# A kernel of attention and a gated product: seven products also in the fourth stay, and kept weight pieces loaded back

## The chip, the cores and the metric

The kernel runs on one core of one Trainium2 chip. The time is the device time of one execution in microseconds. Every number of a profile comes from one profiled execution; it lists the engines TensorE (PE, with its weight loads as PEld), VectorE (DVE), ScalarE (ACT), GpSimd (POOL) and SyncE (SP), whose queue issues nearly all DMAs.

## The reference, cut to what matters

Attention with batch 4, 8 heads, 768 positions and 64 channels a head; a query sees 8 global keys and the last 96 positions, with a bias that falls with the distance. Its result, as 3072 rows x of 512 channels, goes through two products that are multiplied and a third:

```python
scores = scale * np.matmul(q, k.transpose(0, 1, 3, 2)) + bias
a = softmax(np.where(keep, scores, -1e9))
x = matmul(a, v).transpose(0, 2, 1, 3).reshape(3072, 512)
out = (x @ w_a) * (x @ w_b) @ w_out      # w_a, w_b: 512 x 1536; w_out: 1536 x 512
```

The three weights are float64, whose words the kernel turns into float32 on the chip. The products are made in a split form: each float32 operand is cut into a high half that the matmul takes whole and a low half that is the rest, and three matmuls (high x high, low x high, high x low) stand for one product.

## The kernel before, in words

**Tiles.** The 3072 rows are six blocks u of 512. The 1536 inner channels are six sets fp of 256. A set has six pieces of 128 x 512: A11, A12, A21, A22 (columns of w_a and w_b) and O0, O1 (rows of w_out). Attention of a block runs in four granules (scores, exponentials, turned weights through DRAM, values).

**Stays and passes.** Converted weights of a few sets are kept in SBUF for a stay, and blocks pass by them. STAYS and TURNS give 18 passes: stay 1 (sets 0, 1, 2; passes 0 to 2, blocks 0, 1, 2), stay 2 (3, 4; passes 3 to 6), stay 3 (5; passes 7 to 9), stay 4 (sets 5, 2; passes 10, 11, 12 with blocks 3, 4, 5), stay 5 (3, 4; passes 13, 14), stay 6 (0, 1; passes 15 to 17). The sums of a block so far are stored to DRAM (`part`) and loaded when it comes again. Blocks 4 and 5 have none yet in passes 11 and 12.

**A pass.** In the first stay `project_plain` makes the two inner products as they are. From the second on `project` uses a seven-product scheme (Strassen's, in Winograd's form) on quarters of x and of A: seven products of 12 matmuls of 256 columns on the two PSUM banks al and ga, with copies and sums between them on ScalarE and VectorE. Their product h (two tiles of 128 x 512) goes back through w_out. In passes 0 to 12 `back` does it plainly: `cut` makes the halves hh and hl of both tiles (two copies, two subtractions, 512 wide), and 8 x 3 matmuls of 512 columns a set add up in the four banks acc; `evict` takes them out once a pass, with four sums or, for a block with no sums yet, four copies. In passes 13 to 16 (PAIRED), `project(strong=True)` calls `seven`, which makes seven forms of h, each a high and a low part of 256 columns, and four sums between quarters; `strong_back` then does seven products of six matmuls of 256 columns for each set of the pass, on three banks, and adds them to the four quarters of the block's sums, a VectorE sum behind each product. Pass 17 has its own end.

**Where the forms lie.** `room` gives tiles of attention and of the conversions, which are idle by pass 13, to the forms of h (hroom) and of w_out (wroom). `load_o` loads O0 and O1 of a set back and makes seven forms of them. For sets in QUADFPS, `load_w` leaves the O pieces to `load_o`.

**Weights.** `to32` makes a float32 piece of a float64 one: a DMA of 512 KB from wts, two ScalarE operations (L688, L723) and four VectorE operations (L695, L703, L713, L730), into a tile m of which each tag has one copy. For the first stay, `convert_plain` converts the six pieces of sets 0, 1, 2 and splits them straight into their places (`wform` with direct). For later stays `convert` converts all six pieces of a set again, makes the sums S1 to S4 and stores A11, A12, S2, S1, S3, S4, A22, O0, O1 to DRAM (dw); `load_w` loads them (wl) when the stay begins, and splits them. So sets 0, 1 and 2 are converted twice.

**Order.** The plan records every operation, and `order` emits them in the order of ORDER, a list of indices written out in the code. An operation that either engine can do runs on ScalarE where ON_SCALAR names it, else on VectorE. Each engine and SP's queue work through their own operations strictly in this order, and an operation waits for the last user of its tile or bank.

Of the kernel before, what the change touches and what calls it, by code (L numbers as in the profile page):

```python
# [10 lines left out]
F32 = mybir.dt.float32  # L11
F32R = mybir.dt.float32r
# [67 lines left out]
PAIRED = (13, 14, 15, 16)  # L80
LAST = len(PASSES) - 1
QUADFPS = (3, 4, 0, 1)
SEVEN = {13: ("psS", "acc0", "psA"), 14: ("acc1", "acc2", "acc3"), 15: ("psS", "acc0", "psA"), 16: ("acc1", "acc2", "acc3"), 17: ("psS", "acc3", "psA")}
# [15 lines left out]
ROOMAT = 13  # L99
LASTFP = 1  # L100
OADJ = {4: (26612.0, 23990.0), 5: (41063.0, 32495.0)}
BADJ = {13: (-88541.0, -44480.0), 14: (-15687.0, -31498.0), 15: (-69190.0, 137971.0), 16: (-1031.0, -17073.0), 17: (8575.0, 2763.0, 3140.0)}
# [503 lines left out]
class Fast:  # L606
# [144 lines left out]
    def wform(self, fp, name, due, src, direct):  # L751
        if direct:
            w = self.slot(fp, name, 0.0, True)
            self.split(due, lambda: src[:, :], w, lambda: w[:, 1], lambda: w[:, 0], CN, [src])
            return
# [4 lines left out]
    def convert(self, fp, due, step, direct):  # L760
# [5 lines left out]
        def quad(i, name):  # L766
            m[name] = self.to32(fp, i, at[i], "m" + name)
# [1595 lines left out]
```

## Time and profile before

| | |
|---|---|
| median of 3 runs | 688.73 us (687.43 to 692.22) |
| profiled execution | 689.54 us, span 687.8 us |
| TensorE, VectorE, ScalarE busy | 668.1, 636.7, 381.9 us |
| matmuls | 6519 |
| moved by DMA | 164.80 MB |

The span runs from the first to the last instruction; 1.74 us of the execution lie around it. "Busy" counts the time in which at least one instruction of the engine is under way. A matmul's own duration is longer than its distance to the next one, since matmuls are pipelined.

### The profile page before, as it was taken

How to read it: one execution, taken by the hardware profiler on the slowest of the kernel's cores; microseconds unless marked ns; L12 is line 12 of the kernel's file. 1: busy time of each engine (PE TensorE's matmuls, PEld its weight loads, DVE VectorE, ACT ScalarE, POOL GpSimd, SP SyncE). 2: the span in 40 equal slices, each digit the busy share in tenths (PEclk: the TensorE clock that was granted, in tenths of full speed). 3: DMA queues.
4: the chain of work that ended last, by engine and by line, in shares of the span. 5: the costliest groups of instructions: out<-in, count | busy, mean ns of one | idle time of the engine just before them, and what ended most of it. 6: DMA issues, size and time to landing. Idle time of an engine off the chain costs nothing.

```text
span 687.8 us, 17093 instructions
## 1 busy us (share of the span) xinstructions
PE 668.1 (97%) x6519; PEld 606.6 (88%) x6519; DVE 636.7 (93%) x1616; ACT 381.9 (56%) x1029; POOL 10.0 (1%) x32
## 2 busy tenths in 40 slices
PE   5899999999999999999999999999999999999996
PEld 4689797778887999989999998999999999999996
DVE  8999899878799999999989998999989999999996
ACT  8999767564635666634756665344444554554210
POOL 1000000000000000000000000000000000000000
PEclk9999999999999999999999999999999999999999
DMA  8769899989999978899888979966566537522334
GB/s 304 254 227 286 277 260 322 286 272 272 319 277 317 328 233 251 286 280 296 312 268 240 304 245 283 302 239 241 186 226 198 187 108 230 179 69 77 108 108 128
DMA packets 79100, 164.80 MB, mean 240 GB/s; under 512 B 8034, under 2 KB 32738, under 8 KB 77218
## 3 DMA queue, kind: packets, MB, share of 16 engines
q1 hardware_dynamic: 78722, 163.41, 74.6%
q8 instruction: 53, 0.87, 0.5%
q14 instruction: 37, 0.30, 0.1%
q10 hardware_dynamic: 288, 0.22, 0.1%
HBM read 110.65 MB, written 52.95 MB: 238 GB/s over the span
## 4 chain that ended last, share of the span: by engine, by line
PE 77%; DMA 9%; DVE 9%; ACT 3%; issue 1%; SPq 1%; DVEq 0%; ACTq 0%
PE al L1403 21%; PE acc L1593 17%; PE ga L1403 16%; PE m_acc L1650 3%; PE ps L1031 3%; DMA wl_A<-dw_A 2%; PE m_psS L1650 2%; DMA py<-mir 2%; DMA wr<-wts 2%; PE pa L515 2%; DMA X<-dx 1%; ACT t L1015 1%; PE ps_al L515 1%; PE m_psA L1650 1%; DVE t L999 1%
## 5 line engine op out<-in xcount | busy, mean ns | idle before, releaser
L1593 PE MATMUL acc<-w_O,hh 128*128 128x512 f32 x416 | 148.4, 401 | 0.0
L1015 ACT ACTIVATE t<-t,sm 128x168 f32<-128x168 f32 x192 | 81.9, 429 | 29.4 <-DVE sm L999 29.4
L1593 PEld LDWEIGHTS acc<-w_O,hh 128*128 128x128 f32 x416 | 78.2, 188 | 16.1
L1593 PE MATMUL acc<-w_O,hl 128*128 128x512 f32 x208 | 81.9, 394 | 0.0
L1403 PE MATMUL al<-xf_T,w_S 128*128 128x256 f32 x600 | 79.5, 282 | 0.0
L1403 PEld LDWEIGHTS al<-xf_T,w_S 128*128 128x128 f32 x600 | 75.7, 188 | 1.4 <-ACT s L650 0.2
L999 DVE CUSTOM_DVE_ANT_0 t<-ps,mask 128x168 f32<-128x168 f32 x168 | 49.2, 326 | 8.3 <-PE ps L1031 8.1
L650 ACT COPY s<-al 128x512 f32<-128x512 f32 x49 | 28.7, 586 | 49.2 <-PE al L1403 49.1
L688 ACT ACTIVATE wm<-wr 128x512 f32<-128x512 f32 x54 | 35.8, 671 | 15.2 <-DMA wr<-wts 6.8
L1593 PEld LDWEIGHTS acc<-w_O,hl 128*128 128x128 f32 x208 | 39.2, 188 | 5.6 <-DVE hl L660 0.4
L1031 PEld LDWEIGHTS ps<-qk 64*64 64x64 f32 x1008 | 30.6, 139 | 14.8 <-issue 6.6
L1403 PE MATMUL al<-xf_B,w_A 128*128 128x256 f32 x300 | 40.0, 283 | 0.8 <-DVE h L1553 0.8
L1165 DVE STREAM_TRANSPOSE tt<-t 128x512 f32<-128x512 f32 x80 | 39.9, 549 | 0.8 <-ACT t L1135 0.6
L1403 PEld LDWEIGHTS al<-xf_B,w_A 128*128 128x128 f32 x300 | 38.1, 188 | 2.2 <-DVE h L1553 1.1
L1403 PE MATMUL al<-xf_T,w_A 128*128 128x256 f32 x300 | 40.0, 283 | 0.0
L1403 PE MATMUL ga<-xf_B,w_A 128*128 128x256 f32 x300 | 39.9, 282 | 0.0
L1403 PE MATMUL ga<-xf_T,w_S 128*128 128x256 f32 x300 | 39.8, 282 | 0.0
L1403 PE MATMUL ga<-xf_B,w_S 128*128 128x256 f32 x300 | 39.8, 282 | 0.0
L1512 DVE TENSOR_TENSOR s<-ga,s 128x512 f32<-128x512 f32 x54 | 37.0, 685 | 2.8 <-PE ga L1403 2.4
L1135 ACT ACTIVATE t<-t,sm 128x168 f32<-128x168 f32 x100 | 34.8, 424 | 6.9 <-DVE sm L1115 6.8
L1403 PEld LDWEIGHTS al<-xf_T,w_A 128*128 128x128 f32 x300 | 37.8, 188 | 0.9 <-DVE s L1512 0.2
L1031 PE MATMUL ps<-qk 64*64 64x168 f32 (+2 forms) x1008 | 36.0, 273 | 2.7 <-DMA qk<-qf 1.9
(437 smaller groups left out, 1548.6 us busy)
## 6 DMA issues: line engine op xcount, KB each, us to landing
wr<-wts SPq DMA_DIRECT2D x54, 512.0 KB, 5.7
mir<-tt SPq DMA_DIRECT2D x80, 192.0 KB, 4.0
vt<-vd SPq DMA_DIRECT2D x24, 512.0 KB, 6.3
qk<-qk SPq DMA_DIRECT2D x20, 576.0 KB, 6.3
X<-dx SPq DMA_DIRECT2D x11, 1024.0 KB, 6.6
part<-o SPq DMA_DIRECT2D x40, 256.0 KB, 4.0
o<-part SPq DMA_DIRECT2D x36, 256.0 KB, 3.9
px<-mir SPq DMA_DIRECT2D x20, 448.0 KB, 6.8
```

The source lines that it names most:

```text
L515: self.main.nc.tensor.matmul(self.banks[s][64 * h : 64 * h + 64, o : o + 64], self.vt[rows, v0 : v0 + 64], src[rows, 2 * s : 2 * s + 2, 2 ...
L650: self.nc.scalar.copy(out(), src())
L688: lambda e: nc.scalar.activation(m(), high().bitcast(F32), AF.Abs),
L999: lambda e: nc.vector.tensor_tensor_reduce(t[:, i, h], bank[:, c0 : c0 + KW], self.mask[pair][:, h, kind], -0.125, 3.0e38, ALU.add, ALU.mi ...
L1015: lambda e: nc.scalar.activation(t[:, i, h], t[:, i, h], AF.Exp, bias=sm[:, 0, j : j + 1], scale=-1.0, accum_out=sm[:, 1, j : j + 1],),
L1031: nc.tensor.matmul(bank[64 * s : 64 * s + 64, c0 + c : c0 + c + w], qk[rows, q0 + 64 * s : q0 + 64 * s + 64], qk[rows, k0 + k : k0 + k + w ...
L1135: nc.scalar.mul(flat()[:, j], flat()[:, j], sm[:, 3, j : j + 1])
L1165: nc.vector.transpose(dst[:, :, e0 : e0 + n], src[:, :, c0 : c0 + 32 * n].rearrange("p j (e k) -> p j e k", e=n),)
L1403: self.nc.tensor.matmul(bank[:, ab * HT : ab * HT + HT], w[:, a, (2 * ab + c) * P : (2 * ab + c) * P + P], x[:, b, c], start=first, stop=F ...
L1512: lambda e: nc.vector.tensor_tensor(s[:, :], bank[:, :], s[:, :], op=ALU.add),
L1593: self.nc.tensor.matmul(acc[i][:, :], a[:, rows], w[:, b], start=first and f == 0 and k == 0, stop=False, skip_group_check=True,)
L1650: self.nc.tensor.matmul(bank[:, c * HT : c * HT + HT], fa(k, c * P, c * P + P), fb(l), start=first, stop=False, skip_group_check=True,)
```

## The change

PAIRED, QUADFPS and SEVEN take in passes 10, 11, 12 and sets 5 and 2, so these passes use `strong_back` with both sets, and `load_o` makes forms of O for sets 5 and 2. `strong_back` copies the first product of a quarter where the block has no sums yet. `room` is called twice: at pass 10 with attention's tiles, the raw-weight tiles and the tiles o, and at pass 13 with the tiles m; the block's sums now lie in the two query tiles qk0 and qk1 (`outs`, four places). `wform` with direct also stores the piece, so the 18 pieces of sets 0, 1, 2 go to DRAM in the first stay, and `convert` of these sets loads four of them (`again`) and makes and stores only S1 to S4. `back` gets its weights handed in. ORDER and ON_SCALAR are written anew (3240 operations, before 3230).

```diff
@@ -77,10 +77,10 @@
 FLOORS = ((1030.0, 1750.0), (3400.0, 4200.0))
 COLD = (600.0, 600.0)
 LAGGED = (1, 2)
-PAIRED = (13, 14, 15, 16)
+PAIRED = (10, 11, 12, 13, 14, 15, 16)
 LAST = len(PASSES) - 1
-QUADFPS = (3, 4, 0, 1)
-SEVEN = {13: ("psS", "acc0", "psA"), 14: ("acc1", "acc2", "acc3"), 15: ("psS", "acc0", "psA"), 16: ("acc1", "acc2", "acc3"), 17: ("psS", "acc3", "psA")}
+QUADFPS = (5, 2, 3, 4, 0, 1)
+SEVEN = {10: ("acc1", "acc2", "acc3"), 11: ("psS", "acc0", "psA"), 12: ("acc1", "acc2", "acc3"), 13: ("psS", "acc0", "psA"), 14: ("acc1", "acc2", "acc3"), 15: ("psS", "acc0", "psA"), 16: ("acc1", "acc2", "acc3"), 17: ("psS", "acc3", "psA")}
 JOINED = (3, 4, 5)
 JOINT = 3150.0
 BEHIND = 2
@@ -96,10 +96,10 @@
 WRBUFS = 3
 XBUFS = 1
 
-ROOMAT = 13
+ROOMAT = (10, 13)
 LASTFP = 1
-OADJ = {4: (26612.0, 23990.0), 5: (41063.0, 32495.0)}
-BADJ = {13: (-88541.0, -44480.0), 14: (-15687.0, -31498.0), 15: (-69190.0, 137971.0), 16: (-1031.0, -17073.0), 17: (8575.0, 2763.0, 3140.0)}
+OADJ = {3: (0.0, 0.0), 4: (26612.0, 23990.0), 5: (41063.0, 32495.0)}
+BADJ = {10: (0.0, 0.0), 11: (0.0, 0.0), 12: (0.0, 0.0), 13: (-88541.0, -44480.0), 14: (-15687.0, -31498.0), 15: (-69190.0, 137971.0), 16: (-1031.0, -17073.0), 17: (8575.0, 2763.0, 3140.0)}
 
 AHEAD = 0.5
 FORM0 = 30657.0
@@ -123,241 +123,245 @@
 
 
 ORDER = (
...
 )
 
 ON_SCALAR = (
...
 )
 
 
@@ -752,19 +756,25 @@
         if direct:
             w = self.slot(fp, name, 0.0, True)
             self.split(due, lambda: src[:, :], w, lambda: w[:, 1], lambda: w[:, 0], CN, [src])
-            return
         d = self.dram([P, CN], F32, f"dw{fp}_{name}")
         self.saved[fp, name] = d
         self.dma(due + 500.0, lambda: d[:, :], lambda: src[:, :], [src], [d], CN * 4 * P)
 
+    def again(self, fp, piece, name, due):
+        st = self.sbuf([P, CN], F32, "m" + name, f"wlm{fp}_{piece}")
+        d = self.saved[fp, name]
+        self.dma(due - LEADS[2], lambda: st[:, :], lambda: d[:, :], [d], [st], CN * 4 * P, LATES[1])
+        return st
+
     def convert(self, fp, due, step, direct):
         m = {}
         sub = ALU.subtract
 
         at = [due + i * step + CADJ[fp][i] for i in range(6)]
+        kept = (fp, "O0") in self.saved
 
         def quad(i, name):
-            m[name] = self.to32(fp, i, at[i], "m" + name)
+            m[name] = self.again(fp, i, name, at[i]) if kept else self.to32(fp, i, at[i], "m" + name)
 
         def temp(name, a, b, alu, t, out=None):
             o = out or self.sbuf([P, CN], F32, "m" + name, f"wm{fp}_{name}")
@@ -772,9 +782,11 @@
             m[name] = o
 
         quad(0, "A11")
-        self.wform(fp, "A11", at[0], m["A11"], direct)
+        if not kept:
+            self.wform(fp, "A11", at[0], m["A11"], direct)
         quad(1, "A12")
-        self.wform(fp, "A12", at[1], m["A12"], direct)
+        if not kept:
+            self.wform(fp, "A12", at[1], m["A12"], direct)
         quad(2, "A21")
         quad(3, "A22")
         t = at[3]
@@ -786,6 +798,8 @@
         self.wform(fp, "S3", t + 400, m["S3"], direct)
         temp("S4", m["A12"], m["S2"], sub, t + 600, out=m["A12"])
         self.wform(fp, "S4", t + 600, m["S4"], direct)
+        if kept:
+            return
         self.wform(fp, "A22", t + 800, m["A22"], direct)
         for f in range(2):
             w = self.to32(fp, 4 + f, at[4 + f], "mS1")
@@ -796,19 +810,27 @@
             m = self.to32(fp, i, dues[i], "m" + (PLAIN + ("S1",))[i % 5])
             self.wform(fp, name, dues[i], m, True)
 
-    def room(self):
+    def room(self, first):
         sb = self.sbuf
         flat = "p a b c -> p (a b c)"
-        found = [(sb([P, NH, 2, KW], F32, "t", f"ft{k}", TBUFS), flat, 2) for k in range(TBUFS)]
-        found += [(sb([P, 6, 2 * NH * 32], F32, "tt", "ftt", TTBUFS), "p a b -> p (a b)", 3)]
-        found += [(sb([P, 4, 2 * NH, 32], F32, "py0", "fpy"), flat, 2)]
-        found += [(sb([P, VN], F32, "vt", f"fvt{k}", VBUFS), None, 2) for k in range(VBUFS)]
-        found += [(sb([P, 2 * CN], I32, "wraw", f"fwr{k}", WRBUFS), None, 2) for k in range(WRBUFS)]
-        found += [(sb([P, CN], F32, "m" + k, "fm" + k), None, 1) for k in PLAIN + ("S1",)]
-        found += [(sb([P, T], F32R, k, "f" + k, 3), None, 1) for k in ("hh", "hl")]
-        found += [(sb([P, 2, 2, KW], F32, f"mask{p}", f"fm{p}"), flat, 1) for p in range(NPAIR)]
+        if first:
+            found = [(sb([P, NH, 2, KW], F32, "t", f"ft{k}", TBUFS), flat, 2) for k in range(TBUFS)]
+            found += [(sb([P, 6, 2 * NH * 32], F32, "tt", "ftt", TTBUFS), "p a b -> p (a b)", 3)]
+            found += [(sb([P, 4, 2 * NH, 32], F32, "py0", "fpy"), flat, 2)]
+            found += [(sb([P, VN], F32, "vt", f"fvt{k}", VBUFS), None, 2) for k in range(VBUFS)]
+            found += [(sb([P, T], F32R, k, "f" + k, 3), None, 1) for k in ("hh", "hl")]
+            found += [(sb([P, 2, 2, KW], F32, f"mask{p}", f"fm{p}"), flat, 1) for p in range(NPAIR)]
+            found += [(sb([P, 512], F32, "o", f"fo{k}", 3), None, 1) for k in range(3)]
+            found += [(sb([P, 2 * CN], I32, "wraw", f"fwr{k}", WRBUFS), None, 2) for k in range(WRBUFS)]
+            keys = [self.kept(f"qk{k}", f"fqk{k}") for k in range(KBUFS)]
+            self.oroom = [(buf, k) for buf in keys for k in range(2)]
+        else:
+            found = [(sb([P, CN], F32, "m" + k, "fm" + k), None, 1) for k in PLAIN + ("S1",)]
         places = [(buf, flat, k) for buf, flat, n in found for k in range(n)]
-        self.wroom, self.hroom, self.hnext, self.used = places[:7], places[7:], 0, 0
+        if first:
+            self.wroom, self.hroom, self.hnext, self.used = places[:7], places[7:], 0, 0
+        else:
+            self.hroom = self.hroom + places
 
     def place(self, where):
         if where[0] == "w":
@@ -828,6 +850,12 @@
             return whole[:, o + b0 : o + b1].bitcast(F32R)
 
         return at, [(mine, "H"), (buf, (self.used, "H"))], [(mine, "L"), (buf, (self.used, "L"))]
+
+    def outs(self, name):
+        buf, k = self.oroom[self.onext % len(self.oroom)]
+        self.onext += 1
+        mine = self.plan.buf(None, None, F32, f"o{buf.name}_{k}", name)
+        return lambda: buf[:, 512 * k : 512 * k + 512], [mine, (buf, name)]
 
     def form_of(self, due, where, src, reads):
         at, hi, lo = self.place(where)
@@ -1576,7 +1604,7 @@
             parts.append((hh, hl))
         return parts
 
-    def back(self, fp, due, parts, acc, first):
+    def back(self, ws, due, parts, acc, first):
         st = 3 * pe(512)
         if isinstance(due, list):
             at = lambda f, i: due[i // 2] + (2 * f + i % 2) * st
@@ -1584,7 +1612,7 @@
             at = lambda f, i: due + (4 * f + i) * st
         for f in range(2):
             hh, hl = parts[f]
-            w = self.w[fp, f"O{f}"]
+            w = ws[f]
             for i in range(4):
                 rows = slice(i * P, i * P + P)
 
@@ -1615,7 +1643,8 @@
         p, q, r = [self.bank(k, f"m{i}_{k}") for k in SEVEN[i]]
         step = 6 * pe(HT) * len(group)
         out = {}
-        old = self.part[u]
+        old = self.part.get(u)
+        begun = set()
         new = None if last or end else self.part_of(u, due)
         for n, (ci, cj) in enumerate(((0, 0), (0, 1), (1, 1), (1, 0))):
             rows = [2 * ci, 2 * ci + 1]
@@ -1625,15 +1654,17 @@
                 at = lambda rows=rows, cut=cut: end[:, rows[0] : rows[0] + 2, cut]
                 out[ci, cj] = (at, [(end, k) for k in keys])
                 continue
-            o = self.sbuf([P, 512], F32, "o", f"o{i}_{ci}{cj}", 3)
-            at = lambda o=o: o[:, :].rearrange("p (a c) -> p a c", a=2)
-            out[ci, cj] = (at, [o])
+            whole, mine = self.outs(f"o{i}_{ci}{cj}")
+            at = lambda whole=whole: whole().rearrange("p (a c) -> p a c", a=2)
+            out[ci, cj] = (at, mine)
+            if old is None:
+                continue
             self.dma(
                 due + n * step - LEADS[4],
                 at,
                 lambda rows=rows, cut=cut: old[rows[0] : rows[0] + 2, :, cut].rearrange("a p c -> p a c"),
                 [(old, k) for k in keys],
-                [o],
+                mine,
                 512 * 4 * P,
             )
 
@@ -1667,6 +1698,11 @@
 
         def add(n, quad, bank, cut=False):
             at, keys = out[quad]
+            if old is None and quad not in begun:
+                begun.add(quad)
+                src = lambda: bank[:, :].rearrange("p (a c) -> p a c", a=2)
+                self.copy(due + n * step, at, src, 512, [bank], keys, psum=True)
+                return
             if not cut:
                 self.plan.op(
                     due + n * step,
@@ -1877,6 +1913,7 @@
     def run(self):
         self.open()
         self.w, self.saved, self.xsaved, self.part = {}, {}, {}, {}
+        self.oroom, self.onext = [], 0
         fpt = 7 * 12 * pe(HT) + 24 * pe(512)
         more = 12 * pe(HT)
         att = 4 * NPAIR * (2 * 620.0 + 530.0) / 2 * 1.0 + 600.0
@@ -1930,8 +1967,8 @@
             for fp, (a, b) in CONV.items():
                 if i <= a < i + 1:
                     self.convert(fp, at(a), (at(b) - at(a)) / 6, False)
-            if i == ROOMAT:
-                self.room()
+            if i in ROOMAT:
+                self.room(not self.paired)
                 self.paired = True
             if i and PASSES[i - 1][0] != stay:
                 for k, fp in enumerate(fps):
@@ -1957,8 +1994,10 @@
                     prev(due + (96 if plain else 84) * pe(HT))
                 over = k + 1 == len(fps) and (i + 1 in PAIRED or PASSES[i + 1][1] != u)
 
-                def prev(d, fp=fp, parts=parts, acc=acc, first=fresh and k == 0, over=over, u=u, i=i):
-                    self.back(fp, d, parts, acc, first)
+                ws = [self.w[fp, f"O{f}"] for f in range(2)]
+
+                def prev(d, ws=ws, parts=parts, acc=acc, first=fresh and k == 0, over=over, u=u, i=i):
+                    self.back(ws, d, parts, acc, first)
                     d = d[-1] if isinstance(d, list) else d
                     if over:
                         self.evict(u, d + 24 * pe(512), acc, u not in seen, i == last_use[u], None)
```

## Rows read from the trace of the kernel before

**Rows 1.** Table of stretches: us, busy us by engine (instructions), PEclk, DMA share, GB/s.
```profile
10.00:110.00 100.00, 91.69 (x1176) 79.41 (x1168) 96.41 (x293) 83.68 (x260) 2.42 (x8) 1.00 0.84 270
110.00:220.00 110.00, 109.26 (x1033) 86.74 (x1032) 92.85 (x260) 61.42 (x181) 1.67 (x6) 1.00 0.94 297
...
268.00:429.00 161.00, 160.39 (x1762) 147.40 (x1760) 152.28 (x390) 92.78 (x264) 3.35 (x8) 1.00 0.90 280
429.00:541.00 112.00, 111.77 (x790) 103.53 (x791) 105.13 (x205) 46.82 (x89) 0.00 (x0) 1.00 0.69 227
541.00:683.00 142.00, 141.34 (x1185) 140.82 (x1183) 136.43 (x310) 58.70 (x131) 0.00 (x0) 1.00 0.42 132
```

**Rows 2.** Waits of PE, 220 to 690 us: us in total, times, longest.
```profile
PE al L1403 <- DVE h L1553: 0.8, 1, 0.8
```

**Rows 3.** Chain that ended last: start us, us, what; runs of matmuls.
```profile
223.68 3.49 PE acc L1593 x15
...
585.05 2.15 PE m_acc L1650 x18
```

**Rows 4.** Chain that ended last, its longest transfers between 60 and 110 us.
```profile
65.08 7.98 DMA wr<-wts
...
95.10 5.42 DMA mir<-tt
101.53 5.19 DMA py<-mir
```

**Rows 5.** Timeline of PE: pass 10's first product (idle before, and its releaser).
```profile
429.23 0.97 PE L1403 MATMUL al<-xf_B,w_A 128*128 128x256 f32 x6 [0.84 <-DVE h L1553]
```

**Rows 6.** Timeline of DVE: start us, us, instructions; distances from start to start.
```profile
504.36 0.42 DVE L695 TENSOR_SCALAR wm<-wm 128x512 f32<-128x512 f32 x1
504.69 0.42 DVE L652 CAST w_S<-wl_S 128x512 fp32r<-128x512 f32 x1
...
505.59 1.28 DVE L660 TENSOR_TENSOR w_S<-wl_S,w_S 128x512 fp32r<-128x512 f32 x2
506.79 0.69 DVE L660 TENSOR_TENSOR wm<-wm_S,wm 128x512 f32<-128x512 f32 x1
...
521.16 0.75 DVE L660 TENSOR_TENSOR h<-s 128x256 f32<-128x256 f32 x2
521.83 0.68 DVE L1512 TENSOR_TENSOR s<-ga,s 128x512 f32<-128x512 f32 x1
```

**Rows 7.** Groups of DVE, 268 to 429 us, then 429 to 541 us.
```profile
L713 DVE SCALAR_TENSOR_TENSOR wm<-wr,wm 128x512 int32<-128x512 int32 x9 | 6.2, 686 | 0.1
...
L713 DVE SCALAR_TENSOR_TENSOR wm<-wr,wm 128x512 int32<-128x512 int32 x9 | 6.2, 691 | 0.2
```

**Rows 8.** Groups of ACT, whole span: busy us, mean ns, idle before.
```profile
L723 ACT ACTIVATE wr<-wr 128x512 int32<-128x512 uint32 x54 | 36.4, 678 | 1.6 <-DMA wr<-wts 1.6
L688 ACT ACTIVATE wm<-wr 128x512 f32<-128x512 f32 x54 | 35.8, 671 | 15.2 <-DMA wr<-wts 6.8 <-DMA dw_O<-wm 4.2 <-DMA dw_S<-wm 3.1
L650 ACT CAST hh<-h 128x512 fp32r<-128x512 f32 x32 | 19.6, 617 | 9.6 <-PE acc L1593 4.6 <-DVE h L660 4.1 <-DVE h L1553 0.5
L650 ACT CAST fwr<-h 128x256 fp32r<-128x256 f32 x12 | 4.9, 406 | 2.2 <-DVE h L660 1.6 <-DVE h L1553 0.5
```

**Rows 9.** DMA queues: packets, MB, share of 16 engines' span.
```profile
q1 hardware_dynamic: 78722, 163.41, 74.6%
```

**Rows 10.** Waits of ACT for stores of weights: us in total, times, longest.
```profile
ACT wm L688 <- DMA dw_O<-wm: 4.2, 1, 4.2
ACT wm L688 <- DMA dw_S<-wm: 3.1, 2, 2.6
```

**Rows 11.** Table of stretches: the 10 us with the most GB/s.
```profile
210.00:220.00 10.00, 9.74 (x109) 7.88 (x102) 9.06 (x28) 3.25 (x7) 0.00 (x0) 1.00 1.00 358
```

**Rows 12.** Groups of PE's weight loads: busy us, mean ns.
```profile
L1650 PEld LDWEIGHTS m_acc<-w_O,fvt 128*128 128x128 f32 x42 | 5.5, 188 | 0.0
```

468 rows, old and new, of tables (ON_SCALAR, ORDER) are left out of this document.

## The prediction

> **What bounds the kernel now.** I read four views in this order. First the table of stretches. From 110 us on TensorE is busy for 99 to 100% of each stretch, and VectorE for 84 to 96% of it; ScalarE is half idle in the last 260 us [rows 1]. The reader is to see that two engines are nearly full and that only one can be the bound. The waits of TensorE settle which: from 220 us to the end it waits for another engine once, for 0.8 us [rows 2]. So behind 220 us TensorE works through its list without a gap, and an instruction taken out of it there comes off the end time, as long as VectorE still delivers. Third, the chain of waits gives TensorE's pace inside a run of matmuls: 15 of 512 columns take 3.49 us, 0.2327 us each, and 18 of 256 columns take 2.15 us, 0.1194 us each [rows 3]. The busy means are longer, because matmuls overlap; they are not used. The granted clock is 1.00 in all these stretches, the 2.4 GHz level [rows 1]. Fourth, the chain in the first stage, which is another regime: between 60 and 110 us it runs through transfers, among them 7.98, 5.42 and 5.19 us long [rows 4], with the 16 DMA engines busy for 84% of 10 to 110 us [rows 1].
>
> **The products of passes 10 to 12.** Today each pass does two plain products back, 2 x 24 matmuls of 512 columns: 48 x 0.2327 = 11.17 us. Seven products for two sets are 7 x 2 x 6 = 84 matmuls of 256 columns: 84 x 0.1194 = 10.03 us [rows 3]. That saves 1.14 us a pass, **3.4 us** for three. Pass 10 begins at 429.23 us [rows 5], inside the stretch without waits, so all of it counts.
>
> Weighed against a rule: the row has the half-wide matmul at 51% of the wide one. The Trainium skill, TensorE: Matmul & The Clock Gate, section Back-to-back issue gap, gives a stream with weight loads about 131 ns at 512 columns and 81 ns at 128. By it a pass would go from 6.3 us to at least 6.8 us, so the change would add time. The trace disagrees at 512 columns (232.7 ns), and the measurement decides.
>
> **VectorE, passes 10 to 13 (429 to 541 us).** Its pace is again taken from start to start: 0.60 us for a 512-wide sum, 0.335 us for a 256-wide one and for a 512-wide operation without a second tensor [rows 6]. Added: each of six projections cuts seven forms and makes four sums, 11 x 0.335, in place of two cuts of 0.60: 2.49 us, 14.9 us in all. Each seven-product pass adds its banks seven times. Pass 10 had four sums, and passes 11 and 12 had four copies, of which four are copies still; so nine sums more, 5.4 us. The output weights of sets 5 and 2 become seven forms each, 2 x 3.69 us less two cuts of set 2: 6.2 us. Together 26.5 us. Removed: a conversion is two operations of 0.335 and two of 0.60, 1.87 us. Nine of the 18 that go lie between 268 and 429 us and nine behind that [rows 7]: 16.8 us each. So VectorE has net 9.7 us more in 429 to 541 us, where it is busy for 105.1 of 112 [rows 1]. Left where it is, that is 114.8 us in 108.6. But 16.8 us come free just ahead, and weight splits and conversions that lie in this stretch can move there. The order in the diff does so: counted down that list with the paces above, between the first products of passes 10 and 13 stand 82 us of VectorE beside 89 us of TensorE, no denser than today's 105 to 112. I take **0**. The bounds are 0 and 6.2 us (114.8 less 108.6).
>
> **ScalarE.** Added, if it does all of them: high halves, 6 x (7 x 0.41 - 2 x 0.62) + 14 x 0.41 - 2 x 0.62 = 14.3 us [rows 8]. Removed in the same stretch: 9 x (0.67 + 0.68) = 12.1 us [rows 8]. It is busy for 46.8 of 112 us there [rows 1]. I take 0; without that cover it would be 2.2 us.
>
> **Loads in place of conversions, later half.** 18 loads of 512 KB become 12 of 256 KB, 15 stores go, and two loads come for set 5's output pieces. Less traffic, at a DMA share of 0.69 to 0.90 [rows 1]: 0, with a gain excluded since TensorE waits for none of it [rows 2]. SP's queue loses a net 19 issues there, and the first stage gets 18.
>
> **The 18 new stores, in the first stage.** This is the only added work without cover. In the new order they stand between the first granules and the end of the first pass's attention, which I put at 10 to 110 us. 163.41 MB took 74.6% of 687.8 us on the 16 engines [rows 9], 3.14 us a MB; 18 x 0.262 MB are 14.8 us. Free there are 16 us [rows 1], so the share goes from 0.84 to 0.99. Each store also stands on SP's queue behind a conversion that must end first, and loads of queries, values and raw weights queue behind it. A buffer of converted weights has one copy, so the next conversion on ScalarE waits until the store has landed, with attention's exponentials queued behind it, and values behind those. The 54 stores of today cost ScalarE 4.2 + 3.1 = 7.3 us of such waits [rows 10]; 18 in proportion 2.4 us, if all reach the end. For the transfers the near price is the chain: 18.6 us of them between 60 and 110 us [rows 4], lengthened in proportion to the traffic (270 to 317 GB/s [rows 1], 17%) by 3.2 us. Bounds: nothing (a 10 us stretch later moves 358 GB/s [rows 11]) and all 14.8 us in series. A gain is excluded for the stores themselves. I take **1.5 us**, about half of the chain's 3.2, because TensorE's own idle time in the stretch is small and other work stands ready.
>
> Beside that price: the Trainium skill, Perfetto Trace Analysis, section Identifying the Most-Contended Engine, calls the occupancy of the 16 DMA engines misleading and goes by bandwidth. By it 317 against 358 GB/s leaves room, the term is 0, and the sum is 3.4 us faster; the row of the share makes the stage full. No run shows yet which holds.
>
> **Sum.** -3.4 + 1.5 = -1.9 us. The profiled execution took 689.54 us for a span of 687.8; so 687.6 us. It lies 0.8 us above the median of the three runs, and against that median the forecast is **686.8 us**.
>
> **Rivals.**
> 1. *Slower: the stores hold up the start.* Its place is 10 to 110 us, and since TensorE has no slack behind 220 us [rows 2] the whole delay arrives at the end. At its full price, 14.8 - 3.4 = +11.4 us, 700 us; at the chain's 3.2 us and the 2.4 us of buffer waits together, +2.2 us, 691 us. It decides from 3.4 us of delay. For it: the share of 0.84 and a chain through transfers. Against: 358 GB/s were moved elsewhere. Chance 0.17, half of it over 1% slower.
> 2. *VectorE becomes the bound in passes 10 to 13.* Up to 6.2 us late: 6.2 - 3.4 + 1.5 = +4.3 us, 693 us. For it: 541 to 683 us, which already runs seven products, holds VectorE at 96% [rows 1]. Against: just there TensorE waits for nothing. Chance 0.08, within 1%.
> 3. *Faster: the freed 33.7 us of VectorE and 24 us of ScalarE take work out of the first 220 us,* where TensorE is idle for 8.3 + 0.7 us [rows 1]. If half of that goes and the stores are hidden: -3.4 - 4.5 = -7.9 us, 681 us. Against: the first conversion that goes lies behind 268 us, so only work moved later helps. Chance 0.10, 0.04 of it over 1%.
> 4. *The half-wide matmul costs more than half.* If each went at the busy time of its weight load, 188 ns [rows 12], a pass would take 15.8 us, +4.6; three passes +13.9 us, 703 us. Against: 18 in 2.15 us [rows 3]. Chance 0.02. The Trainium skill, TensorE: Matmul & The Clock Gate, section Back-to-back issue gap, points this way, as said above.
>
> **The numbers.** The forecast has 0.63. About 1% (6.9 us) is what a measurement of this kernel can tell from no change: below 681.8 is faster, above 695.6 slower. Faster 0.04 (rival 3), slower 0.08 + 0.02 = 0.10, same 0.86. The range of 8 in 10: the low end is the full 3.4 us and some of rival 3, with 1.3 us for the lowest run against the median, 682.5; the high end takes in rival 2 and the mild half of rival 1, 693.
>
> **What would show it.** Right: 84 matmuls a pass at 0.119 us in passes 10 to 12, 36 conversions in place of 54, TensorE still without waits behind its first plain products, and pass 10's first product within some 2 us of 429.23. Wrong: that product later by over 3.4 us, with transfers longer in the chain ahead of 110 us (rival 1); waits of TensorE for VectorE's forms or sums between 429 and 541 us (rival 2); that product clearly earlier (rival 3).

## The result and the profile after

The changed kernel takes 695.42 us (median of 11 runs, 692.76 to 700.15) where the kernel before takes 688.73 us on the same chip (11 runs, 686.31 to 693.40). The ratio is 1.0089, interval 1.0064 to 1.0114: slower by 6 us, where the forecast was 686.8 us. The profiled execution took 695.42 us for a span of 693.6.

The table of stretches of the kernel after, to be read beside [rows 1]:

```profile
10.00:110.00 100.00, 91.30 (x1157) 79.10 (x1149) 94.01 (x306) 83.19 (x260) 3.80 (x8) 0.98 0.93 296
110.00:220.00 110.00, 109.18 (x1051) 87.64 (x1052) 90.99 (x244) 60.29 (x181) 2.25 (x6) 1.00 0.93 292
268.00:429.00 161.00, 161.00 (x1663) 148.64 (x1663) 151.21 (x366) 80.12 (x222) 2.55 (x6) 1.00 0.85 265
429.00:541.00 112.00, 107.27 (x871) 103.78 (x871) 102.18 (x238) 48.91 (x116) 0.66 (x1) 0.97 0.54 168
541.00:683.00 142.00, 141.48 (x1181) 140.59 (x1180) 136.42 (x314) 61.80 (x141) 0.00 (x0) 1.00 0.42 127
```

Only one row has changed much: from 429 to 541 us TensorE is busy for 107.27 us of 112 instead of 111.77, and the granted clock is 0.97 on average. TensorE's busy time in the first 110 us, where the forecast put its one price, is the same to 0.4 us, although the DMA share rose from 0.84 to 0.93 and the traffic from 270 to 296 GB/s. The waits of PE from 220 us on, which answer to [rows 2] (us in total, times, longest), name what is new:

```profile
PE m_acc L1681 <- DVE fpy L656: 2.9, 1, 2.9
PE ga L1431 <- ACT s L654: 0.7, 1, 0.7
PE pa L538 <- DVE xf_T L664: 0.4, 1, 0.4
PE al L1431 <- ACT s L654: 0.4, 1, 0.4
```

One wait of 2.9 us for a form of h on VectorE leads. Around it, the timeline of PE (start us, us, instructions, idle time before and its releaser):

```profile
459.23 1.58 PE L1431 MATMUL ga<-xf_B,w_A 128*128 128x256 f32 x12
463.76 1.90 PE L1681 MATMUL m_acc<-w_O,fpy 128*128 128x256 f32 x6 [2.94 <-DVE fpy L656]
465.95 1.65 PE L1681 MATMUL m_acc<-ft,fvt 128*128 128x256 f32 x6 [0.29 <-DVE o L1855]
467.39 2.75 PE L1431 MATMUL al<-xf_B,w_A 128*128 128x256 f32 x12
```

These are the first products back of pass 10. After 2.94 us without work, 24 matmuls of 256 columns take from 463.76 to 469.95 us, 6.2 us instead of 24 x 0.119 = 2.9 (a second wait of 0.29 us lies in them). The table of stretches says why: the granted clock is at half, the 1.2 GHz level.

```profile
464.00:470.00 6.00, 5.71 (x25) 5.24 (x26) 5.83 (x18) 0.41 (x1) 0.00 (x0) 0.50 0.56 175
```

So the place costs 2.9 us of waiting and 3.3 us of slow work, 6.2 together. The timeline of DVE shows VectorE idle all the while:

```profile
462.87 0.29 DVE L656 CAST fvt<-h 128x256 fp32r<-128x256 f32 x1 [5.96 <-issue]
463.42 0.29 DVE L656 CAST fpy<-h 128x256 fp32r<-128x256 f32 x1
```

Its row names no releaser ("issue"). The timeline of ACT does:

```profile
457.82 0.59 ACT L654 COPY vt<-pa 128x512 f32<-128x512 f32 x1 [4.89 <-PE pa L538]
459.43 0.37 ACT L654 COPY sa<-al 128x256 f32<-128x256 f32 x1 [1.03 <-PE al L1431]
462.54 0.41 ACT L654 CAST fvt<-h 128x256 fp32r<-128x256 f32 x1 [2.74 <-DMA dx<-vt]
```

And the timeline of SP's queue has the store that it names:

```profile
458.43 0.32 SPq L644 DMA_DIRECT2D dx<-vt  x1
458.80 2.53 SPq L644 DMA_DIRECT2D out<-o  x2
```

ScalarE's cast into fvt waits for the store dx<-vt, and VectorE's cast into another fvt starts 0.33 us after it. fvt is a half of vt, attention's tile for values. `room` hands out the places for the forms of h in the order of a list, and its first entries are tiles of attention: py0, then vt. Behind the changed pass 10 that list is used while attention's last granule is not done. VectorE's idle time has two parts: the granule's values come first, and then their store. The values leave the bank into vt at 457.82, the store is issued at 458.43 and lands some 4 us later, and only then may a form be written there. The form fpy, for which TensorE waits, stands behind the fvt cast in VectorE's order. That the store is what holds VectorE is read here from ScalarE's row; experiments 1 and 2 test it.

In the kernel before, the same granule's values come at 443.81 us, inside pass 10 too, but the first form of h is needed in pass 13: attention's tiles had long been free.

The products are as forecast. The chain of waits of the kernel after has the matmuls of the new products at the pace of [rows 3], 18 in 2.15 us:

```profile
470.15 2.15 PE m_acc L1681 x18
472.30 1.43 PE ga L1431 x12
473.73 1.42 PE m_acc L1681 x12
```

The groups of PE show 480 wide matmuls in the products back; the kernel before had 624 (416 and 208):

```profile
L1621 PE MATMUL acc<-w_O,hh 128*128 128x512 f32 x320 | 114.8, 403 | 0.0
L1621 PE MATMUL acc<-w_O,hl 128*128 128x512 f32 x160 | 62.9, 393 | 0.0
```

The groups of ACT show 36 conversions for the 54 of [rows 8]:

```profile
L727 ACT ACTIVATE wr<-wr 128x512 int32<-128x512 uint32 x36 | 24.2, 676 | 2.5 <-DMA wr<-wts 2.5
```

And pass 10's first product (timeline of PE) is not late; it starts 2.3 us earlier than in [rows 5], with 1.2 us less work done by then (one granule of values, 1.9 us, comes later, and three wide matmuls, 0.7 us, earlier):

```profile
426.94 1.59 PE L1431 MATMUL al<-xf_B,w_A 128*128 128x256 f32 x12
```

### The profile page after: what moved, and what is told of

Its sections match the earlier page's. It is cut to its first block, busy times and chain, and to the rows that moved or that the text cites. A ratio compares the mean times of both kernels' runs of the same rounds, so it can differ in the third digit from the quotient of the medians.

```text
span 693.6 us, 17311 instructions
## 1 busy us (share of the span) xinstructions
PE 669.3 (96%) x6627; PEld 613.3 (88%) x6627; DVE 630.8 (91%) x1633; ACT 371.7 (54%) x1026; POOL 12.0 (2%) x32
## 4 chain that ended last, share of the span: by engine, by line
PE 70%; DVE 15%; DMA 5%; ACT 4%; issue 4%; SPq 1%; POOL 0%; DVEq 0%; ACTq 0%; POOLq 0%
PE al L1431 18%; PE acc L1621 13%; PE ga L1431 13%; PE m_acc L1681 5%; PE ps L1059 3%; DMA py<-mir 2%; PE m_psS L1681 2%; DVE s L1540 2%; PE pa L519 2%; PE ps_al L519 1%; DVE h L664 1%; ACT t L1043 1%; DMA mir<-tt 1%; DVE qk L1709 1%; DVE w_O L664 1%
## 5 line engine op out<-in xcount | busy, mean ns | idle before, releaser
L1621 PE MATMUL acc<-w_O,hh 128*128 128x512 f32 x320 | 114.8, 403 | 0.0
L1621 PEld LDWEIGHTS acc<-w_O,hh 128*128 128x128 f32 x320 | 60.1, 188 | 13.1 <-DVE o L1855 0.3
L1621 PE MATMUL acc<-w_O,hl 128*128 128x512 f32 x160 | 62.9, 393 | 0.0
L1431 PEld LDWEIGHTS ga<-xf_B,w_S 128*128 128x128 f32 x300 | 37.7, 188 | 1.4 <-ACT s L654 0.9
L1431 PEld LDWEIGHTS ga<-xf_B,w_A 128*128 128x128 f32 x300 | 37.5, 188 | 0.9 <-DVE s L1540 0.4
L1431 PEld LDWEIGHTS ga<-xf_T,w_S 128*128 128x128 f32 x300 | 37.7, 188 | 0.6 <-DVE s L1540 0.2
```

The costliest lines, as they stand in the source:

```text
L1431: self.nc.tensor.matmul(bank[:, ab * HT : ab * HT + HT], w[:, a, (2 * ab + c) * P : (2 * ab + c) * P + P], x[:, b, c], start=first, stop=F ...
L1621: self.nc.tensor.matmul(acc[i][:, :], a[:, rows], w[:, b], start=first and f == 0 and k == 0, stop=False, skip_group_check=True,)
```

## The experiments

Ratios are to the kernel before on the same chip, with 95% intervals; the experiments were spread over four chips. A profile shows one execution, which can lie some us from the median: that of experiment 1 took 693.03 us (median 690.20), that of experiment 7 took 699.40 (median 702.93).

**1. The late tiles at the end of the list of places.** In `room`, the same places in another order, no operation moved:

```diff
             found += [(sb([P, 6, 2 * NH * 32], F32, "tt", "ftt", TTBUFS), "p a b -> p (a b)", 3)]
-            found += [(sb([P, 4, 2 * NH, 32], F32, "py0", "fpy"), flat, 2)]
-            found += [(sb([P, VN], F32, "vt", f"fvt{k}", VBUFS), None, 2) for k in range(VBUFS)]
+            found += [(sb([P, 2 * CN], I32, "wraw", f"fwr{k}", WRBUFS), None, 2) for k in range(WRBUFS)]
...
+            found += [(sb([P, 4, 2 * NH, 32], F32, "py0", "fpy"), flat, 2)]
+            found += [(sb([P, VN], F32, "vt", f"fvt{k}", VBUFS), None, 2) for k in range(VBUFS)]
```

> The changed kernel, with only the list of places for the forms of h in another order: raw-weight tiles, masks, halves and sum tiles first, attention's tiles py and vt last. The same operations in the same order on every engine. Theory A (the first forms of pass 10 stand in tiles that attention's last granule still uses, so VectorE stands for 6.0 us at 456.9 to 462.9 us behind the store of vt, and TensorE behind it): that wait goes, TensorE's waits behind 220 us fall from 5.2 to under 1.5 us, its clock stays at 1.00 between 460 and 470 us, and the time falls by 6.5 to 8.5 us from 695.4, to 687 to 689 us: ratio to the kernel before 0.997 to 1.001. Rival B (VectorE has too much to do in passes 10 to 13): another wait takes its place within 30 us, and the time stays at 693 to 696 us, ratio 1.006 to 1.011.

Measured: 690.20 us, ratio 0.9993 (0.9966 to 1.0020). Theory A's ratio held. Against 1.0089 this is 1.0%, 6.6 us back, and the long wait is gone. The waits of PE from 220 us on:

```profile
PE ga L1431 <- ACT s L654: 0.7, 1, 0.7
PE acc L1621 <- DVE o L1855: 0.5, 1, 0.5
PE al L1431 <- DVE xf_T L664: 0.3, 1, 0.3
PE ga L1431 <- DVE s L1540: 0.2, 1, 0.2
```

And of the table of stretches the row of passes 10 to 13:

```profile
429.00:541.00 112.00, 110.77 (x919) 107.62 (x918) 107.57 (x256) 52.46 (x126) 0.27 (x1) 1.00 0.55 175
```

The granted clock stays at 1.00. From the first product of pass 10 to that of pass 13, the same work on every engine, the changed kernel takes 98.27 us and this one 91.45, 6.8 us less. The row of the changed kernel:

```profile
426.94:525.21 98.27, 93.53 (x755) 90.05 (x754) 89.49 (x211) 41.67 (x99) 0.66 (x1) 0.97 0.51 159
```

That of this experiment:

```profile
431.29:522.74 91.45, 90.22 (x755) 87.51 (x754) 88.61 (x210) 41.27 (x98) 0.27 (x1) 1.00 0.52 168
```

What follows: the 6 us are the wait for a place and the slow work behind it, as the trace had it.

**2. Only vt moved.** py0 stays at the head of the list, vt goes to its end.

> The changed kernel with only vt moved to the end of the list of places; py stays the first place. Theory A with the store of vt as the holder: nearly the whole gain of the run with both moved, since py's last reader (the values product, which ended at 457.4 us) frees py 5.4 us before the store of vt lands (462.8 us); ratio to before 0.997 to 1.003. If py's reader holds as well (its form is also a first one), 2 to 4 us of the loss stay: ratio 1.003 to 1.007. Rival B: 1.006 to 1.011.

Measured: 689.74 us, ratio 0.9993 (0.9961 to 1.0025), the same as with all of the list turned. vt and its store alone held VectorE; py0, whose form was first in the list, did not.

**3. The 18 stores alone, in the kernel before.** Second conversions and plain products stay; the first conversions' pieces are stored as well, and nobody reads them.

```diff
             self.split(due, lambda: src[:, :], w, ...)
+            d = self.dram([P, CN], F32, f"dk{fp}_{name}")
+            self.dma(due + 500.0, lambda: d[:, :], lambda: src[:, :], [src], [d], CN * 4 * P)
             return
```

> The kernel before, with nothing but the 18 stores of the first sets' pieces added, at the places on SP's queue that the changed kernel gives them (its products, its second conversions and the rest of the order as before). The prediction's term: +1.5 us, bounds 0 and 14.8 us. Theory now (the changed kernel has done as much by its pass 10 as the kernel before at the same time, so the stores are hidden): -1 to +1.5 us, ratio 0.999 to 1.002. Rival 1 of the prediction (the stores hold up the start): +3 us or more, ratio over 1.004.

Measured: 706.30 us, ratio 1.0227 (1.0187 to 1.0266). My theory's number failed; a price like the first rival's is real here, 16 us. The waits of ACT for stores from 10 to 220 us, which answer to the 7.3 us of [rows 10]:

```profile
ACT wm L677 <- DMA dk_A<-wm: 18.0, 4, 7.5
ACT wm L677 <- DMA dw_O<-wm: 4.0, 1, 4.0
```

Those of SP's queue for VectorE's last conversion step, in this experiment:

```profile
SPq L670 <- DVE wm L719: 22.4, 11, 5.4
```

In the kernel before, also from 10 to 220 us:

```profile
SPq L681 <- DVE wm L730: 31.6, 15, 4.9
```

And those of PE from 60 to 220 us:

```profile
PE al_1(0,)_999 L1415 <- ACT s_1(1,)_970 L639: 4.7, 1, 4.7
PE pa L504 <- DMA py<-mir: 3.4, 1, 3.4
```

ScalarE's next conversion waits for a store to land (the buffer has one copy): with 0.4 us for other stores 22.4 us, 15.1 more than before, and TensorE waits for ScalarE's copies. SP's queue also stands in front of stores whose conversion is not done, but it did so longer before, so that wait does not explain the loss. Between 60 and 110 us TensorE is busy for 41.87 us instead of 48.31, and the DMA engines are less busy, not more. The row of that stretch in this experiment:

```profile
60.00:110.00 50.00, 41.87 (x435) 37.20 (x434) 38.90 (x112) 33.11 (x99) 0.70 (x3) 0.90 0.78 244
```

In the kernel before:

```profile
60.00:110.00 50.00, 48.31 (x590) 41.95 (x589) 46.85 (x128) 35.16 (x103) 1.26 (x3) 1.00 0.94 276
```

That speaks for the places of the stores in the order, and against busy DMA engines, as the price. The edit does not separate the two fully: the stores move other transfers as well.

**4. Stored pieces loaded back, plain products kept.** The kernel before with the 18 stores added, and with the 18 second conversions and their 15 stores taken out for 12 loads; so the change without its products.

```diff
-            m[name] = self.to32(fp, i, at[i], "m" + name)
+            m[name] = self.again(fp, i, name, at[i]) if kept else self.to32(fp, i, at[i], "m" + name)
```

> The kernel before with the other half of the change alone: the 18 pieces are stored and loaded back and the second conversions of sets 0, 1, 2 and their 15 stores are gone; the products of passes 10 to 12 stay plain, and the order is that of before with the gone operations taken out. TensorE's work is that of before. Theory (TensorE is the bound behind 220 us, so 33.7 us less of VectorE and 24 us less of ScalarE bring nothing there): within 1.5 us of before, ratio 0.998 to 1.002. Rival 3 of the prediction (freed work lets the first 220 us close up): 3 us or more faster, ratio under 0.996.

Measured: 701.55 us, ratio 1.0156 (1.0119 to 1.0192). Neither number held. Less work than in experiment 3, and still slow; behind the first 220 us TensorE waits for nothing, so the loss lies in them, and the freed work of VectorE and ScalarE brings nothing behind them, as the theory said. The waits of ACT ahead of 220 us:

```profile
ACT wm L669 <- DMA dw_A<-wm: 13.4, 2, 11.4
```

In the order of before, the stores hold the conversions up again.

**5. The first variant without the stores.** Experiment 1 with 17 of the 18 stores left out; the loads all read the one piece that is stored, so the numbers computed are not the reference's.

```diff
+        if direct and self.saved:
+            self.saved[fp, name] = self.saved[0, "A11"]
+            return
         d = self.dram([P, CN], F32, f"dw{fp}_{name}")
```

> Left out: 17 of the 18 new stores of converted pieces; the later loads all read the one piece that is still stored, so the outputs are not the reference's. Everything else, order included, is e1_late_tiles_last. Theory (the stores cost what is left of the saving): the first variant stood at 0.9993 of the kernel before where the products alone should give 688.7 - 3.4 = 685.3 us, 0.995; so without the stores 0.995 (0.993 to 0.997), and TensorE's clock in 20 to 40 us back to 1.00. Rival (the stores are hidden in the rewritten order, and the rest is small waits behind 430 us and the new order of the start itself): 0.998 to 1.001, clock in 20 to 40 us still near 0.91.

Measured: 690.04 us, ratio 1.0005 (0.9980 to 1.0030). My theory was wrong here and the rival right: in the rewritten order the stores cost nothing that can be measured (the two intervals together leave room for some 1.7 us), and the saving of the products is not hidden behind them. TensorE's clock of 0.91 between 20 and 40 us (1.00 in the kernel before) stayed as it was, so it belongs to the new order of the start, not to the stores.

**6 and 7. The stores on GpSimd's queue,** first in experiment 1's kernel, then in experiment 3's.

```diff
+        q = self.nc.gpsimd if direct else None
-        self.dma(due + 500.0, ..., [src], [d], CN * 4 * P)
+        self.dma(due + 500.0, ..., [src], [d], CN * 4 * P, queue=q)
```

> e1_late_tiles_last with the 18 new stores issued from GpSimd's queue instead of SyncE's; nothing is left out. Theory (the stores cost time because they stand in SyncE's queue in front of loads: 20.6 us of SyncE's waits in the first 220 us stand at store issues behind VectorE's last conversion step): 0.994 to 0.997, a version faster than both. Rival (their price, if any, is the traffic and the single copy of the conversion buffers): 0.998 to 1.001 as before the move.

> e2_stores_alone with its 18 stores issued from GpSimd's queue instead of SyncE's. That variant was 1.0227: in its trace ScalarE's first conversion step waits 18.0 us (4 times) for the landing of a store, and SyncE's store issues wait 22.4 us for VectorE's last conversion step. Theory (buffer: a store that lands late holds the only copy of the buffer, and attention's exponentials queue behind ScalarE's wait): GpSimd's queue issues the stores at once, they land within some 3 us of the conversion, most of the 18 us of waits go too, so that queue and buffer are one chain: 1.000 to 1.008. Rival (the traffic itself, 4.7 MB in a stretch whose transfers are already near 0.95 of the DMA engines' time): 1.015 to 1.025 as before the move.

Measured: 696.16 us, ratio 1.0111 (1.0072 to 1.0150), and 702.93 us, ratio 1.0200 (1.0165 to 1.0236). In the rewritten order neither number held: the other queue is a loss of 1.2%. The waits of ACT from 10 to 220 us show the stores holding the conversions, 11.8 us; in experiment 1 ScalarE had waited there for one store, 2.4 us:

```profile
ACT wm L693 <- DMA dw_A<-wm: 11.8, 3, 5.9
```

In the order of before the rival's number held. The waits of ACT in that kernel:

```profile
ACT wm L678 <- DMA dk_A<-wm: 8.9, 3, 5.2
```

Half of ScalarE's waits for these stores are gone. By the medians little of the time went with them (706.30 to 702.93 us), but the profiled execution is the fastest of its kernel: 699.40 us, 8.1 less than the profiled one of experiment 3. So the trace fits the chain through the buffer, and the medians do not decide between it and the traffic. What is shown: the other queue does not bring back the time in either order. Why it makes the waits in the rewritten order longer is not settled.

**8 and 9. Casts of forms moved to ScalarE.** Experiment 1 with 32 casts (8), then with all 50 operations that either engine can do (9) behind pass 10 added to ON_SCALAR.

> e1_late_tiles_last with the 32 casts of forms (high halves) behind pass 10 that VectorE still does given to ScalarE; nothing is left out and no place in the order changes. That variant has done the 3.3 us less of products and yet stands at 0.9993; in its trace VectorE is busy for 18.79 of 20, 11.90 of 12 and 107.57 of 112 us behind pass 10's first product, and TensorE has small waits there for sums and forms. Theory (VectorE's load behind 430 us gives the saving back, the second rival in a mild form): VectorE loses 32 x 0.285 = 9.1 us, TensorE's waits behind 430 us go, 0.994 to 0.997. Rival (the small waits hang on latencies between the engines, not on VectorE's load; a cast takes 0.41 us on ScalarE and queues there): 0.998 to 1.003, the waits only change their names.

> The same with all 50 operations of that stretch that either engine can do given to ScalarE (beside the 32 casts of forms: 7 casts of activations and of output weights' halves more, 5 of those, copies out of banks, one scaling): VectorE 13 us less, ScalarE some 19 us more, of which it has 260 - 110 = 150 free. Theory (VectorE's load): no worse than e8_forms_scalar, 0.993 to 0.996. Rival (latencies): 1.000 to 1.006, with TensorE waiting for ScalarE in place of VectorE.

Measured: 695.90 us, ratio 1.0107 (1.0084 to 1.0130), and 696.63 us, ratio 1.0100 (1.0079 to 1.0120). Both theories failed; the rival's direction, and worse than it said. Of experiment 8 the row from the first product of pass 10 to that of pass 13, to be read beside experiment 1's:

```profile
427.76:524.20 96.44, 91.50 (x755) 87.85 (x754) 85.90 (x196) 45.32 (x112) 0.40 (x1) 1.00 0.51 159
```

And its waits of PE from 430 us on:

```profile
PE al L1419 <- ACT s L642: 1.5, 2, 1.3
PE ga L1419 <- DVE s L1528: 1.1, 1, 1.1
PE m_acc L1669 <- DVE o L1843: 0.9, 1, 0.9
```

For the same products VectorE is busy for 2.7 us less (85.90 against 88.61) and ScalarE is half idle, yet they take 5.0 us longer (96.44 against 91.45). The load of VectorE alone is not what counts. The waits name copies and sums that are ready late; that the time until they are ready is the cause fits these rows, but no run isolates it.

**10. Casts of forms moved to VectorE.** The opposite, for 23 casts between the first products of passes 11 and 13.

> The opposite of e8_forms_scalar: e1_late_tiles_last with the 23 casts of forms that ScalarE does between the first products of passes 11 and 13 given to VectorE; nothing is left out. Theory (what counts there is how soon a form is ready, not VectorE's load): a cast takes 0.285 us on VectorE instead of 0.41 and needs no hand-over, 0.996 to 0.999, the small waits behind 450 us shorter. Rival (VectorE is full too in these 60 us, 58.4 of 60 busy, so that both engines stand at their balance): 23 x 0.285 = 6.6 us more work against 1.6 us of idle time, +5 us, 1.005 to 1.009, with TensorE waiting for VectorE's sums.

Measured: 693.03 us, ratio 1.0060 (1.0036 to 1.0084), as the rival said. The same row of experiment 10, again to be read beside experiment 1's:

```profile
426.14:520.13 93.99, 91.43 (x756) 87.92 (x754) 92.40 (x231) 33.82 (x75) 0.40 (x1) 1.00 0.51 162
```

And the first of PE's waits in experiment 10, from 430 us on:

```profile
PE al L1416 <- DVE s L1525: 2.1, 5, 0.6
```

The same products take 2.5 us longer, and VectorE is busy for 92.40 of the 93.99 us: it has no room left either. With experiments 8 and 9: with every operation left at its place in the order, moving casts costs either way. Whether another order would give the saving back is not tested.

No version beat the kernel before. Experiments 1, 2 and 5 equal it.

## Why the prediction was wrong

**The step that failed** is the one on VectorE in passes 10 to 13, which ends in "I take 0". It counted the work of the new forms and sums and asked whether VectorE has the time. It did not ask where the forms are put and until when that place is taken. The diff shows it: ROOMAT goes from 13 to (10, 13), so `room`'s list, headed by tiles of attention, is used three passes earlier, and attention's last granule lies in pass 10. The second rival was near by its place, and by its sign (waits for VectorE's forms between 429 and 541 us) the trace would have passed for it, but its mechanism was another: at that wait VectorE was not overfull, it stood idle for 5.96 us. Measured price: 6.2 us in the trace, 6.6 us by experiments 1 and 2.

**The products.** Right as work: 84 matmuls a pass at the pace of [rows 3], 3.4 us less on TensorE's list. 18 matmuls of 256 columns take 2.15 us in the products of pass 10 too, 119 ns each, 51% of the 232.7 ns at 512 columns. The figures of the Trainium skill that spoke against it (TensorE: Matmul & The Clock Gate, section Back-to-back issue gap) do not hold for these matmuls.

**VectorE's bounds, 0 to 6.2 us.** Zero was the wrong end even without the wait for a place, since experiments 1 and 5 show no gain at the end: 0.995 lies outside both intervals. The step to zero also compared two measures: 82 us summed from paces against 105 us of busy time, hence "no denser". In busy time, between the first products of passes 10 and 13, VectorE has 86.72 of 91.72 us before and 88.61 of 91.45 in experiment 1, so it did become denser. The kernel before:

```profile
429.23:520.95 91.72, 91.72 (x662) 85.38 (x663) 86.72 (x162) 37.12 (x68) 0.00 (x0) 1.00 0.72 237
```

Two landmarks place the loss, the first products of passes 10 and 13. That of pass 13 in the kernel before (timeline of PE; that of pass 10 is [rows 5]):

```profile
520.95 0.76 PE L1403 MATMUL al<-xf_B,w_A 128*128 128x256 f32 x5
```

Both in experiment 1:

```profile
431.29 1.60 PE L1431 MATMUL al<-xf_B,w_A 128*128 128x256 f32 x12
...
522.74 1.59 PE L1431 MATMUL al<-xf_B,w_A 128*128 128x256 f32 x12
```

Between them stand, by the two lists of order, 504 half-wide and 126 wide matmuls and one granule of values before, and 666, 24 and two granules in the variant. At 0.1194, 0.2327 and 1.9 us that is 91.4 and 88.9 us of work; the times are 91.72 and 91.45. So 0.3 us are lost before and 2.6 in the variant. From pass 13 on it is 161.6 us of work in 166.85 (to the end of the span) against 161.9 in 168.56: 1.4 us more lost. Together 3.7 us, about what the products save. The profile of experiment 2 repeats it (91.75 and 168.42 us); that of experiment 5 has 91.43 and 170.35, so the second part moves by some 2 us between profiles. Named waits cover 1.7 us of it; most of the rest lies in gaps of some 0.1 to 0.25 us that no row names. That VectorE and ScalarE deliver too late is what experiments 8 to 10 support; they don't split the 3.7 us further, and the cause of this part is argued, not shown.

**The stores, 1.5 us.** Not seen in the order that the change brings: experiment 5 against experiment 1 shows no price (1.0005 against 0.9993, intervals of 0.25% to 0.3%), though 1.5 us lie just within what these intervals allow. The working behind it priced the traffic (14.8 us of DMA time, a chain 17% slower), and experiment 3 lost 16 us with the DMA engines less busy. What grew there were ScalarE's waits for stores, by 15.1 us where the prediction had 2.4 in proportion. In the changed kernel's order they nearly vanish; from 10 to 220 us:

```profile
ACT wm L692 <- DMA dw_O<-wm: 0.6, 1, 0.6
```

The Trainium skill (Perfetto Trace Analysis, section Identifying the Most-Contended Engine) goes by bandwidth and calls occupancy misleading; the changed kernel agrees as far as it goes: 296 GB/s and a share of 0.93 in 10 to 110 us had no price that can be measured.

**The other terms.** Loads in place of conversions at 0: no wait of TensorE for them. ScalarE at 0: TensorE's waits for its copies `s` (0.7 us in experiment 1) are part of the 3.7 us.

**The sum again:** -3.4 (products) + 3.7 (sums and forms ready late) + 0 (stores) + 6.2 (the place) = +6.5 us, where 3.7 and 6.2 are read from these traces after the fact; measured +6.1 by the ratio, +6.7 by the medians.

**The rivals.** The first was a mechanism for another kernel: stores hold up the start where they are put into an order as it is (experiments 3 and 4) and not where the order is rewritten around them. The third, freed work closing up the start, did not show: TensorE is busy for 91.30 of 100 us there instead of 91.69, and experiment 4 has no gain behind 220 us. The fourth is refuted by the pace. The sign of a late first product, which the prediction would have read as the first rival, would have misled: this landmark lies at 426.94 us in the changed kernel and at 431.29 in experiment 1, which have the same operations in the same order up to there, and the later one is the faster kernel. One profile does not carry a difference of a few us in the start.

## What to carry to other kernels

When a change makes something be written earlier, price the place as well as the work: list who used that buffer last, when that user's own last store lands, and what stands behind the writer on its engine. And before a wait is called a cause, look for the same wait in the kernel before. Put the tiles that come free last at the end of a list of places; that costs nothing and was worth 6.6 us here. And work taken off a full TensorE need not come off the end: here 3.4 us of it did not, most likely because the engines that feed it were nearly full too.

## What the runs showed of the hardware

A wait of 2.94 us on TensorE in a stretch that was full before and after it was followed by some 6 us at half the granted clock (0.50 from 464 to 470 us), so that the wait cost twice its length. In the same passes TensorE's waits of at most 0.7 us in experiment 1, and of at most 1.3 us in experiment 8, left the clock at 1.00.

An engine's row can say "issue" for a long wait whose cause stands on another engine's row: VectorE's 5.96 us had no releaser, ScalarE's 2.74 us beside it named the store.
